# One core, attention then a relu² feed-forward: raw-weight loads of items 2 to 8 issued by GpSimd, and one accumulator of the last half kept in two PSUM tiles

## The chip, the core and the metric

The kernel runs on one core of a Trainium2 chip. The metric is device microseconds of one execution, lower is better. The three runs of the kernel before gave 591.52, 594.09 and 588.73 us, median 591.52 us. The profiled execution took 588.6 us.

Five engines work side by side: PE (TensorE: matrix products), DVE (VectorE), ACT (ScalarE), POOL (GpSimd) and SP (SyncE, which in this kernel issues every transfer). Each runs its own list of instructions in order, and waits at an instruction whose inputs or buffers are not ready. "SPq" in the profile is the issuing of a transfer.

## The reference

Attention over 4 batches, 8 heads, 768 positions of 64 features, with keys within a window of 16 positions and 24 block summaries (the maximum of each 32 keys; the mean of each 32 values). Its output, 3072 tokens of 512 features, goes through a feed-forward network of 2048 hidden features:

```
scores = concat(where(|i-j| < 16, q k^T / 8, -1e9), q ksum^T / 8 + log 32)
x = softmax(scores) @ concat(v, vsum)            # 3072 x 512
h = x @ w_in                                     # w_in 512 x 2048, float64
g = max(h, 0) ** 2
out = g @ w_out                                  # w_out 2048 x 512, float64
```

## The kernel before

**Tokens.** A group is 64 tokens of one batch (all heads): 48 groups. Eight groups make a unit of 512 tokens: 6 units. A group's attention is scores on PE (`S`, line 647), a maximum, exponential and normalisation on DVE and ACT (lines 739, 778, 797), a transposition, and the product with the values (line 854), which leaves x in `xh` and `xl`, a rounded high part and the remainder. The first eight groups take buffers that later hold weights (`qvpa_lent`, `fv_lent`).

**Block maxima of the keys.** `kb` holds 24 block maxima and then the keys. Scores read one run of columns, the maxima followed by 94 keys, so for each group POOL copies the maxima in front of the next window (`move`, line 660; called KC below). The scores of group g+1 read `kb` and wait for the KC of group g, which itself waits for the scores of group g. POOL also copies the value means into the value buffers of groups 0, 1, 6 and 7 (`copy_s`, line 605; called LS).

**Weights.** The 2048 hidden features are 16 items of 128. For an item, `convert` (lines 953 to 1021) loads 512 KB of w_in and 512 KB of w_out as raw 64-bit words (`load`, line 983: `raw<-wW`), and makes two float32 parts of each on chip: ACT line 986, DVE line 989 and line 995, ACT line 1000, DVE line 1003, whose output `w` PE reads. Items 0 to 2 are converted in two halves, the others whole. The raw words of items 6 to 15 lie in buffers that the first groups' attention used.

**Feed-forward.** Units 0 and 1 go item by item: `h = x w_in` on PE (line 1050, 12 matmuls), relu and square, then `o += g w_out` (line 1074, 12 matmuls). Units 2 and 3, and then 4 and 5, are computed with seven products for each 2 x 2 block in place of eight (`products(0, ...)` and `products(1, ...)`; line 1454). In `products` each of the seven steps j runs over 8 pairs of items and adds into a PSUM accumulator `o` of 128 x 2 x 512 (d = 0 and 1 are its halves of 512 columns, a PSUM bank each). The list `bank` says which accumulator step j uses. Steps 4 and 6 share the last one, `acc[4]`: step 4 fills it, DVE adds it to `u3` and the sum leaves (C22), step 6 adds eight pairs more, and DVE adds it to `u2` (C12, line 1400), whose two halves are the last two transfers of the program (line 1393). The very last pair of step 6 issues the three matmuls of d = 0 first, then the three of d = 1.

**Order.** A planner in Python (`Plan.order`) fixes the order of every engine's list ahead of time from estimated costs and due times (`due`, `begin`). A load is a task of SP there. All tasks are emitted in the planner's order, each on the engine that its lambda calls.

**Transfers.** SP's transfers use eight completion semaphores in turn, and the list makes each wait for the one eight before it. At most eight are therefore under way, and one that is not done holds back the ninth and all behind it.

Of the kernel before, what the change touches and what calls it, by code (L numbers as in the profile page):

```python
# [77 lines left out]
class Slots:  # L78


    def __init__(self, pool, tag, n, tiles=None):
        self.pool, self.tag, self.n, self.tiles = pool, tag, n, tiles
        self.taken, self.made = [], 0
# [21 lines left out]
class Part:  # L105
# [5 lines left out]
    @property  # L111
    def tile(self):
        x = self.buf.tile[:, self.a : self.b]
        return x.rearrange("p (a b) -> p a b", a=self.shape[1]) if self.shape else x
# [14 lines left out]
        return self.of(self.buf.tile)  # L129


class Task:
    def __init__(self, name, engine, cost, emit, key, after, take, use, size, begin):
        self.name, self.engine, self.cost, self.emit, self.key = name, engine, cost, emit, key
        self.after, self.size, self.begin = after, size, begin
        self.take, self.use = ([getattr(b, "buf", b) for b in x] for x in (take, use))


class Plan:
# [101 lines left out]
def attention_then_relu2_ffn(  # L241
# [9 lines left out]
    nc = tc.nc  # L251
# [3 lines left out]
    NT, DM = out.shape  # L255
# [21 lines left out]
    kinds = {}  # L277
# [61 lines left out]
    X_BY = 8  # L339
    SUMS = 274.9, 290.4, 308.3, 379.4, 174.9, 349.5, 257.2, 275.6, 114.0, 167.1, 155.4, 203.9, 122.9, 186.0, 213.8, 213.7  # L340
    BY_POOL = (1, 2, 4, 5,)
    PRODUCT_STEP = 1.56, 1.56, 1.46
    A0, A1, B0, B1 = 12.0, 2.0, 21.0, 2.2
    HALF_AT = 25.0, 32.0
# [2 lines left out]
    unit_at, products_at, at = [], [], T0  # L347
# [605 lines left out]
    def convert(f, ns):  # L953

        k = len(ns)  # L960
        due = at_item[0, f] + (LAG * STEP if ns == (1,) else 0)
        if f < HALVED:
            due = HALF_AT[0] + 0.5 * (f * SLOW + (LAG * STEP if ns == (1,) else 0))
        name = f"{f}" if k == 2 else f"{ns[0]}_{f}"

        raw = buf(f"w{name}", 1, (P, k * DM), I64, f"raw{name}")
        w = buf(f"w{name}", 1, (P, 2 * k * DM), F32R, f"w{name}")
        t = buf("t", 3, (P, 2 * DM), F32, f"t{name}")

        def temp():  # L970
            return t.tile[:, : k * DM]

        def words(i):
            return raw.tile.bitcast(U32).rearrange("p (c w) -> p c w", w=2)[:, :, i]

        def part(i, x):
            return x.rearrange("p (n w c) -> p n w c", n=k, w=2)[:, :, i]

        def by_n(x):
            return x.rearrange("p (n c) -> p n c", n=k)  # L980

        def load(i):
            nc.sync.dma_start(out=raw.tile[:, i * DM : (i + 1) * DM], in_=wW[ns[i], f])

        def rebias():
            nc.scalar.activation(temp(), words(1).bitcast(F32), AF.Prelu, scale=REBIAS, alpha=-SIGN)

        def rest():
            nc.vector.tensor_scalar(
                out=words(0), in0=words(0), scalar1=29, scalar2=None, op0=ALU.logical_shift_right  # L990
            )

        def join():
            x = temp().bitcast(U32)
            nc.vector.scalar_tensor_tensor(
                out=x, in0=x, scalar=3, in1=words(0), op0=ALU.logical_shift_left, op1=ALU.bitwise_or
            )

        def high():
            nc.scalar.copy(out=part(0, w.tile), in_=by_n(temp()))  # L1000

        def low():
            nc.vector.tensor_tensor(  # L1003
                out=part(1, w.tile), in0=by_n(temp()), in1=part(0, w.tile).bitcast(F32), op=ALU.subtract
            )

        t1 = []
        for i in range(k):
            t1.append(add(
                f"WL{ns[i]}_{f}", "SP", 0.45, lambda i=i: load(i), due - 14, take=[raw] * (not i), use=[raw] * i,  # L1010
                behind=t1[0] if i else None, size=P * 4096, begin=due - 31,
            ))
        t2 = add(f"WM{name}", "ACT", 0.02 + 0.5 * k, rebias, due - 8, t1, take=[t], use=[raw])
        t_WM.append(t2)
        t3 = add(f"WR{name}", "DVE", 0.09 + 0.27 * k, rest, due - 8, t1, use=[raw])
        t4 = add(f"WJ{name}", "DVE", 0.03 + 0.54 * k, join, due - 7, [t2, t3], use=[raw, t])
        t6 = add(f"WH{name}", "ACT", 0.08 + 0.43 * k, high, due - 6, [t4], take=[w], use=[t])
        t7 = add(f"WW{name}", "DVE", 0.07 + 0.53 * k, low, due - 4.5, [t6], use=[w, t])
        for i, n in enumerate(ns):
            t_W[n, f] = [t6, t7]  # L1020
            w_parts[n, f] = [Part(w, j * DM, (j + 1) * DM) for j in (2 * i, 2 * i + 1)]
# [351 lines left out]
    even, sums = {}, {}  # L1373

    def products(s, todo):

        if todo[0][:2] == (0, 0):
# [3 lines left out]
            if s:  # L1381
                sums[s][-1].update({("before", k): mixed_end[k] for k in range(2)})
        *acc, u2, u3, made = sums[s]
        bank = acc[0], acc[1], acc[2], acc[3], acc[4], acc[3], acc[4]

        def by_two(x):
# [2 lines left out]
        def leave(name, x, i, j, due, deps, d=slice(0, 2)):  # L1389
            c0 = s * 2 * TU + j * TU  # L1390
            rows = rest_out[i * HALF : (i + 1) * HALF, c0 : c0 + TU].rearrange("(d p) t -> p d t", p=P)
            add(
                f"PS{name}", "SP", 0.45, lambda: nc.sync.dma_start(out=rows[:, d], in_=by_two(x)[:, d]), due, deps, use=[x],
                size=(d.stop - d.start) * 4 * P * DM, begin=due - 20,
            )

        def plus(name, to, o, x, key, deps, take=(), d=slice(0, 2)):
            made[name] = add(
                f"{name}_{s}_{d.start}", "DVE", 0.13 + 0.56 * (d.stop - d.start),
                lambda: nc.vector.tensor_tensor(out=by_two(to)[:, d], in0=o.tile[:, d], in1=by_two(x)[:, d], op=ALU.add),  # L1400
                key, deps, take=take, use=[o, x] + [to] * (not take),
            )
            return made[name]

        for j, p, due in todo:
            o = bank[j]
# [4 lines left out]
            kind, c = ORDER[j]  # L1411
            x, ins, op = (
                (first, None, None), (second, None, None), (first, (last, first), ALU.add), (last, None, None),
                (diff, None, None), (second, (second, first), ALU.subtract), (diff, (first, diff), ALU.add),
            )[j]
# [7 lines left out]
                    out=chunk.tile.bitcast(F32), in_=of[c].rearrange("p w x -> p (w x)")  # L1423
# [4 lines left out]
            if op is not None:  # L1428
# [8 lines left out]
                take=[gh], use=[x], behind=last_of("gh", None) if n or s else t_FI[PLAIN, NF - 1],  # L1437
# [4 lines left out]
                    out=gl.tile, in0=x.tile, in1=gh.tile.bitcast(F32), op=ALU.subtract  # L1442
# [16 lines left out]
            for i, piece in enumerate((todo[::2], todo[1::2]) if end else (todo,)):  # L1459
                t_p = add(  # L1460
                    f"FP{s}_{n}_{i}", "PE", 0.2268 * len(piece), lambda piece=piece, mm=mm: mm(piece), due + 0.1 * i,
                    [t_h, t_l, t_c] + after, take=[o] * begins, use=[chunk, gh, gl] + [o] * (not begins),
                    behind=last_of("product", None),
                )
                last_of("product", t_p)
                if end:
                    d = slice(i, i + 1)
# [5 lines left out]
            if j == 0:  # L1473
                made["U1"] = add(
                    f"U1_{s}", "ACT", 0.97, lambda o=o: nc.scalar.copy(out=by_two(u2), in_=o.tile), due, [t_p], take=[u2], use=[o]
                )
            elif j == 1:
                x = buf("t", 3, (P, 2 * DM), F32, f"c11_{s}")
                leave(f"11_{s}", x, 0, 0, due + 1, [plus("C11", x, o, u2, due, [t_p, made["U1"]], [x])])
            elif j == 2:  # L1480
                plus("U2", u2, o, u2, due, [t_p, made["C11"]])
            elif j == 3:
                last_of("w1_1", plus("U3", u3, o, u2, due, [t_p, made["U2"]], [u3]))
            elif j == 4:
                leave(f"22_{s}", u3, 1, 1, due + 1, [plus("C22", u3, o, u3, due, [t_p, made["U3"]])])
                made["before", 5] = [made["U3"]]
            elif j == 5:
                x = buf("t", 3, (P, 2 * DM), F32, f"c21_{s}") if s else Buf(kinds["w1_2"], (P, 2 * DM), F32, f"c21_{s}")
                leave(f"21_{s}", x, 1, 0, due + 1, [plus("C21", x, o, u2, due, [t_p, made["U2"]], [x])])
                made["before", 6] = [made["C22"]]  # L1490
            elif not end:
                leave(f"12_{s}", u2, 0, 1, due + 1, [plus("C12", u2, o, u2, due, [t_p, made["C21"]])])

# [311 lines left out]
    for u in range(PLAIN + 2):  # L1805
# [14 lines left out]
        if u > PLAIN:  # L1820
            at, rest = unit_at[u], [(j, p) for j in range(SOON, PRODUCTS) for p in range(NQ)]
# [13 lines left out]
        o = [o_buf(f"o{u}_{t}") for t in range(NTT // 2)]  # L1835
# [76 lines left out]
```

## Time and profile before

| what | value |
|---|---|
| median of 3 runs | 591.52 us (588.73 to 594.09) |
| profiled execution | 588.6 us |
| its span, first to last instruction | 586.8 us |
| PE busy, share of the span | 573.3 us, 98% |
| DVE | 443.9 us, 76% |
| ACT | 353.0 us, 60% |
| POOL | 99.2 us, 17% |
| mean granted TensorE clock | 1.000 |
| moved by the transfers | 149.63 MB, 255 GB/s on average |

The 1.8 us between the span and the profiled execution's time lie outside the first and last instruction. PE is busy almost throughout, so the time is PE's work plus the places where PE waits. The profile names, for a wait, the instruction that ended it.

### The profile page before, as it was taken

The page shows a single profiled execution, that of the slowest core. Times are in us where ns is not written, and L with a number is a line of the kernel's source. Part 1 is how long each engine was busy: PE and PEld are TensorE (multiplying, and loading weights), DVE is VectorE, ACT ScalarE, POOL GpSimd, SP SyncE. Part 2 cuts the span into 40 slices and gives each one's busy share as a digit, 9 for nine tenths or more (in the row PEclk, how much of TensorE's full clock was granted, in tenths as well). Part 3 has the DMA queues.
Part 4 walks back from the last instruction along what each step waited for, and adds up shares of the span by engine and source line. Part 5 has one row for each costly group of instructions (what it writes and reads, how often), then busy time and mean ns, then how long its engine had stood idle before and what let it go on. Part 6 is the DMA issues. An engine that isn't in the chain of part 4 may idle for free.

```text
span 586.8 us, 12058 instructions
## 1 busy us (share of the span) xinstructions
PE 573.3 (98%) x4084; PEld 467.0 (80%) x4084; DVE 443.9 (76%) x1018; ACT 353.0 (60%) x876; POOL 99.2 (17%) x165
## 2 busy tenths in 40 slices
PE   8999999999999999999999999999999999999996
PEld 6787878777788888888778888888878888888885
DVE  5999899578457647765986877999968966769863
ACT  2999877667646646465754566676746424654442
POOL 4300005073568004420120022000000000000000
PEclk9999999999999999999999999999999999999999
DMA  8998885869998796996979945999885456667672
GB/s 313 324 394 304 304 301 161 289 214 336 356 325 261 235 332 201 322 320 185 268 248 296 363 153 183 295 303 287 271 268 178 122 158 194 197 187 232 196 225 99
DMA packets 120273, 149.63 MB, mean 255 GB/s; under 512 B 10556, under 2 KB 79164, under 8 KB 120212
## 3 DMA queue, kind: packets, MB, share of 16 engines
q1 hardware_dynamic: 120212, 148.86, 78.0%
q8 instruction: 33, 0.54, 0.4%
q14 instruction: 28, 0.23, 0.1%
HBM read 103.99 MB, written 44.04 MB: 252 GB/s over the span
## 4 chain that ended last, share of the span: by engine, by line
PE 71%; DMA 14%; DVE 5%; SPq 3%; ACT 3%; issue 2%; POOL 2%; DVEq 0%; ACTq 0%
PE o L1454 26%; PE h L1340 15%; PE o L1074 8%; PE o L1647 6%; DMA raw<-wW 6%; PE h L1050 6%; PE sz L1647 4%; PE x L854 3%; PE att L647 2%; DMA qvpa_lent<-vF 2%; DMA turn<-a 2%; DMA a<-turn 1%; PE att L1647 1%; DMA fv_lent<-vS 1%; DMA scr_i<-w 1%
## 5 line engine op out<-in xcount | busy, mean ns | idle before, releaser
L1454 PE MATMUL o<-gh,w 128*128 128x512 f32 x448 | 121.5, 393 | 0.0
L1436 ACT CAST gh<-g 128x512 fp32r<-128x512 f32 x112 | 68.5, 621 | 54.4 <-PE o L1454 25.2
L1454 PEld LDWEIGHTS o<-gh,w 128*128 128x128 f32 x448 | 83.1, 188 | 18.4 <-ACT gh L1436 0.8
L1441 DVE TENSOR_TENSOR gl<-g,gh 128x512 fp32r<-128x512 f32 x112 | 76.5, 695 | 20.9 <-ACT gh L1436 20.6
L1050 PE MATMUL h<-xh,w 128*128 128x512 f32 x240 | 75.0, 392 | 1.2 <-DVE w L1003 0.9
L1454 PE MATMUL o<-gl,w 128*128 128x512 f32 x224 | 69.5, 391 | 0.0
L1340 PE MATMUL h<-xh,w 128*128 128x512 f32 x224 | 69.1, 390 | 0.0
L1074 PE MATMUL o<-w,gh 128*128 128x512 f32 x240 | 62.2, 395 | 1.4 <-ACT gh L1061 1.2
L778 ACT ACTIVATE p<-p,small 128x118 f32<-128x118 f32 x160 | 61.0, 386 | 1.1 <-DVE small L721 0.7
L1050 PEld LDWEIGHTS h<-xh,w 128*128 128x128 f32 x240 | 44.7, 188 | 12.2 <-DVE w L1003 1.7
L1074 PEld LDWEIGHTS o<-w,gh 128*128 128x128 f32 x240 | 44.3, 188 | 11.8 <-ACT gh L1061 1.9
L1454 PEld LDWEIGHTS o<-gl,w 128*128 128x128 f32 x224 | 41.8, 188 | 9.6 <-DVE gl L1441 0.9
L1340 PEld LDWEIGHTS h<-xh,w 128*128 128x128 f32 x224 | 42.0, 188 | 9.1 <-ACT r L1350 0.4
L1050 PE MATMUL h<-xl,w 128*128 128x512 f32 x120 | 46.7, 389 | 0.0
L1340 PE MATMUL h<-xl,w 128*128 128x512 f32 x112 | 43.6, 389 | 0.0
L1350 ACT ACTIVATE r<-h 128x512 f32<-128x512 f32 x32 | 19.1, 596 | 37.1 <-PE h L1340 36.9
L660 POOL COPY kb<-kb 128x96 f32<-128x96 f32 x25 | 8.6, 343 | 193.3 <-ACT kw L672 70.9
L1064 DVE TENSOR_TENSOR gl<-r,gh 128x512 fp32r<-128x512 f32 x30 | 23.2, 774 | 20.3 <-ACT gh L1061 16.9
L721 DVE CUSTOM_DVE_ANT_0 p<-att,mask 128x118 f32<-128x118 f32 x152 | 33.1, 275 | 2.6 <-PE att L647 2.5
L1074 PE MATMUL o<-w,gl 128*128 128x512 f32 x120 | 33.6, 389 | 0.0
L1431 DVE TENSOR_TENSOR g<-g 128x512 f32<-128x512 f32 x48 | 32.8, 689 | 0.4
L778 ACT ACTIVATION_READ_ACCUMULATOR p<-p,small 128x1 f32 x160 | 30.4, 190 | 0.0
(209 smaller groups left out, 1077.7 us busy)
## 6 DMA issues: line engine op xcount, KB each, us to landing
raw<-wW SPq DMA_DIRECT2D x32, 512.0 KB
w<-scr_s SPq DMA_DIRECT2D x64, 256.0 KB
w<-scr_a SPq DMA_DIRECT2D x48, 256.0 KB
turn<-a SPq DMA_DIRECT2D x40, 256.0 KB
a<-turn SPq DMA_DIRECT2D x160, 64.0 KB
scr_t<-ci SPq DMA_DIRECT2D x32, 256.0 KB
w<-scr_i SPq DMA_DIRECT2D x32, 256.0 KB
w<-scr_t SPq DMA_DIRECT2D x32, 256.0 KB
```

The costliest lines, as they stand in the source:

```text
L721: nc.vector.tensor_tensor_reduce(out=pr.tile[:, j, :KEYS], in0=score_at(g, 0, j), in1=mask_of(g)[0], scale=-SCALE, scalar=-NEG, op0=ALU.ad ...
L778: nc.scalar.activation(x, score_tile(g, p % parts)[:, p] if by_pe else x, AF.Exp, bias=nm.tile[:, p : p + 1], scale=SCALE if by_pe else -1 ...
L1050: nc.tensor.matmul(cut(h), lhsT=lhs.tile[:, k * P : (k + 1) * P], rhs=rhs[:, k, c0 : c0 + n], start=(i == 0), stop=(i == 3 * KT - 1),)
L1064: lambda: nc.vector.tensor_tensor(out=cut(gl), in0=cut(r), in1=cut(gh).bitcast(F32), op=ALU.subtract),
L1074: nc.tensor.matmul(o_of(o, t), lhsT=terms[i][0].tile[:, (t - t0) * P : (t - t0 + 1) * P], rhs=terms[i][1].tile, start=(first and i == 0), ...
L1340: nc.tensor.matmul(h.tile, lhsT=lhs.tile[:, k * P : (k + 1) * P], rhs=rhs[:, k, c0 : c0 + TU], start=(i == 0), stop=(i == 3 * KT - 1),)
L1350: t2 = add(f"RL{name}", "ACT", 0.56, lambda: nc.scalar.activation(r.tile, h.tile, AF.Relu), due + 2 - R_LEAD, [t1], take=[r], use=[h])
L1431: lambda x=x, ins=ins, op=op: nc.vector.tensor_tensor(out=x.tile, in0=ins[0].tile, in1=ins[1].tile, op=op),
L1436: f"GH{s}_{n}", "ACT", 0.54, lambda x=x, gh=gh: nc.scalar.copy(out=gh.tile, in_=x.tile), due - GH_LEAD, ready,
L1441: lambda x=x, gh=gh, gl=gl: nc.vector.tensor_tensor(out=gl.tile, in0=x.tile, in1=gh.tile.bitcast(F32), op=ALU.subtract),
L1454: nc.tensor.matmul(o.tile[:, d], lhsT=chunk.tile[:, w * HALF + d * P : w * HALF + (d + 1) * P], rhs=y.tile, start=begins and w == 0 and y ...
L1647: nc.tensor.matmul(o.tile, lhsT=lhs(w, k), rhs=y[k], start=begins and i == 0, stop=i == 5, skip_group_check=not begins,)
```

## The change

There are two edits.

First, the transfers `raw<-wW` of items 2 to 8 (14 transfers of 512 KB) are issued by POOL and no longer by SP. In the planner they are still tasks of SP, so the order in which all tasks are emitted stays, and each of the 14 falls into POOL's list at the place that its emission gives it, between POOL's own copies. They use other completion semaphores than SP's.

Second, in `products(1, ...)` the accumulator of steps 4 and 6 consists of two PSUM tiles of 128 x 512, the two tiles that held the scores (`att`), in place of one tile of 128 x 2 x 512. The addition C22 becomes two instructions of 512 columns in place of one of 1024; C12 had two already.

```
+class Banks:
+    def __init__(self, bufs):
+        self.bufs = bufs
+    @property
+    def tile(self):
+        return self
+    def __getitem__(self, at):
+        d = at[1]
+        if isinstance(d, int):
+            return self.bufs[d].tile
+        assert d.stop == d.start + 1
+        return self.bufs[d.start].tile.unsqueeze(1)
...
+    RAW_BY_POOL = 2, 9
...
         def load(i):
-            nc.sync.dma_start(out=raw.tile[:, i * DM : (i + 1) * DM], in_=wW[ns[i], f])
+            (nc.gpsimd if RAW_BY_POOL[0] <= f < RAW_BY_POOL[1] else nc.sync).dma_start(out=raw.tile[:, i * DM : (i + 1) * DM], in_=wW[ns[i], f])
...
         *acc, u2, u3, made = sums[s]
+        if s and len(acc) == 6:
+            acc[4:] = [Banks([Buf(kinds["atts"], None, None, f"acc{s}_{d}") for d in range(2)])]
+            sums[s] = [*acc, u2, u3, made]
         bank = acc[0], acc[1], acc[2], acc[3], acc[4], acc[3], acc[4]
...
             elif j == 4:
-                leave(f"22_{s}", u3, 1, 1, due + 1, [plus("C22", u3, o, u3, due, [t_p, made["U3"]])])
-                made["before", 5] = [made["U3"]]
+                ds = [slice(d, d + 1) for d in range(2)] if s else [slice(0, 2)]
+                t_22 = [plus("C22", u3, o, u3, due, [t_p, made["U3"]], d=d) for d in ds]
+                leave(f"22_{s}", u3, 1, 1, due + 1, t_22)
+                made["before", 5], made["22"] = [made["U3"]], t_22
...
-                made["before", 6] = [made["C22"]]
+                made["before", 6] = made["22"]
```

On POOL, early in the program: in the rows, `kb<-kb` is a KC, `qvpa_lent<-fv_lent` an LS, and a number behind a name tells buffers apart (line numbers of the changed kernel are 19 or 22 higher). Before:

```order
L605 COPY qvpa_lent<-fv_lent 24x512
L660 COPY kb<-kb 128x4x24 x2
L605 COPY qvpa_lent<-fv_lent 24x512 x2
L660 COPY kb<-kb 128x4x24 x2
L710 MEMSET p_83 128x4x10
```

Now, from the same place:

```order
L679 COPY kb<-kb 128x4x24 x2
L1002 DMA raw_2_477<-wW 128x512
L624 COPY qvpa_lent<-fv_lent 24x512
L1002 DMA raw_496<-wW 128x512
L624 COPY qvpa_lent<-fv_lent 24x512
L1002 DMA raw_496<-wW 128x512
L1002 DMA raw_2_520<-wW 128x512
L1002 DMA raw_525<-wW 128x512
L679 COPY kb<-kb 128x4x24
L1002 DMA raw_525<-wW 128x512
L679 COPY kb<-kb 128x4x24
L729 MEMSET p_83 128x4x10
```

The first pair of `kb` copies are the KC of groups 4 and 5. Five transfers (item 2's two, item 3's two, one of item 4's) now stand between the KC of group 5 and that of group 6, and a sixth between those of groups 6 and 7. The other eight come later: two behind the KC of group 8, six behind that of group 9.

On SP, at the corresponding place, before:

```order
L983 DMA raw_1_459<-wW 128x512
L595 DMA v_80<-vF 128x512
L983 DMA raw_2_477<-wW 128x512
L595 DMA v_81<-vF 128x512
L983 DMA raw_496<-wW 128x512 x2
L983 DMA raw_2_520<-wW 128x512
L983 DMA raw_525<-wW 128x512 x2
L595 DMA v_82<-vF 128x512
L588 DMA q_617<-qW 128x256
```

Now:

```order
L1002 DMA raw_1_459<-wW 128x512
L614 DMA v_80<-vF 128x512
L614 DMA v_81<-vF 128x512
L614 DMA v_82<-vF 128x512
L607 DMA q_617<-qW 128x256
```

The loads of values and queries follow one another, and the same holds further down, up to the raw words of item 9, which SP still issues. On DVE, at the last additions, the rows before end in

```order
L1441 TENSOR_TENSOR gl_52_6397<-g_4_5171,gh_52_6395 128x512
L1441 TENSOR_TENSOR gl_53_6407<-g_5_5205,gh_53_6405 128x512
L1441 TENSOR_TENSOR gl_54_6417<-g_6_5274,gh_54_6415 128x512
L1441 TENSOR_TENSOR gl_55_6427<-g_7_5294,gh_55_6425 128x512
L1400 TENSOR_TENSOR u_1_5908<-o_66,u_1_5908 128x512 x2
```

and now in

```order
L1463 TENSOR_TENSOR gl_52_6398<-g_4_5171,gh_52_6396 128x512
L1463 TENSOR_TENSOR gl_53_6408<-g_5_5205,gh_53_6406 128x512
L1463 TENSOR_TENSOR gl_54_6418<-g_6_5274,gh_54_6416 128x512
L1463 TENSOR_TENSOR gl_55_6428<-g_7_5294,gh_55_6426 128x512
L1422 TENSOR_TENSOR u_1_5908<-att_68,u_1_5908 128x512
L1422 TENSOR_TENSOR u_1_5908<-att_69,u_1_5908 128x512
```

The two last additions read a tile each, and each has a wait for PE of its own; before, both read one tile, and the first waited for all of PE's work on it. PE's list is the same but for the names of the tiles that steps 4 and 6 write.

More of the change, by code (lines that the diff above doesn't have):

```diff
@@ L135, in __init__ @@
         self.after, self.size, self.begin = after, size, begin
-        self.take, self.use = ([getattr(b, "buf", b) for b in x] for x in (take, use))
+        self.take, self.use = ([getattr(c, "buf", c) for b in x for c in getattr(b, "bufs", (b,))] for x in (take, use))
 class Plan:
```

## The prediction

> **What bounds the kernel now.** I read the busy times by stage first, then who waits for whom on PE, then the order of time around PE's waits. Columns of the stages: busy us (instructions) on PE, weight loads, DVE, ACT, POOL, then granted clock, share of the transfer engines, GB/s.
>
> ```profile
> 0.00:20.00 20.00, 17.36 (x244) 13.44 (x244) 12.61 (x28) 7.83 (x31) 9.66 (x45) 1.00 0.92 327
> 20.00:40.00 20.00, 18.12 (x311) 15.57 (x312) 19.42 (x65) 19.28 (x72) 3.40 (x9) 1.00 0.96 356
> 40.00:60.00 20.00, 19.81 (x95) 15.87 (x97) 19.62 (x29) 19.19 (x37) 0.00 (x0) 1.00 0.93 323
> 60.00:80.00 20.00, 19.78 (x142) 16.10 (x135) 17.81 (x41) 14.72 (x34) 0.00 (x0) 1.00 0.92 322
> 200.00:300.00 100.00, 100.00 (x698) 81.41 (x697) 68.86 (x184) 56.15 (x152) 21.49 (x29) 1.00 0.85 274
> 560.00:587.00 27.00, 22.38 (x99) 18.20 (x97) 13.25 (x19) 8.73 (x14) 0.00 (x0) 1.00 0.49 157
> ```
>
> PE is full in the middle, where nothing but its own work counts. From 20 to 60 us DVE, ACT and the transfers are full as well: what is lost there on one of them has no slack to come out of.
>
> ```profile
> span 586.8 us, 12058 instructions
> PE 573.3 (98%) x4084; PEld 467.0 (80%) x4084; DVE 443.9 (76%) x1018; ACT 353.0 (60%) x876; POOL 99.2 (17%) x165
> ```
>
> All PE idle time is 586.8 - 573.3 = 13.5 us, and a good part of it lies before the first operands and behind the last matmul; that caps any gain.
>
> ```profile
> PE x L854 <- DMA a<-turn: 1.9, 3, 1.3
> PE o L1074 <- ACT gh L1061: 1.2, 1, 1.2
> PE h L1050 <- DVE w L1003: 0.9, 2, 0.7
> ```
>
> PE never waits for `raw<-wW` directly. It reaches PE through DVE's `w`, and that wait is 0.9 us in all, twice:
>
> ```profile
> 76.19 0.50 PE L1050 MATMUL h<-xh,w 128*128 128x512 f32 x1 [0.22 <-DVE w L1003]
> 82.59 0.50 PE L1050 MATMUL h<-xh,w 128*128 128x512 f32 x1 [0.66 <-DVE w L1003]
> ```
>
> **Edit 2, the end: -0.60 us.** The last rows before, on PE, DVE and SP:
>
> ```profile
> 581.31 0.39 PE L1454 MATMUL o<-gl,w 128*128 128x512 f32 x1
> 581.99 0.39 PE L1454 MATMUL o<-gl,w 128*128 128x512 f32 x1
> 582.41 1.29 DVE L1400 TENSOR_TENSOR u<-o,u 128x512 f32<-128x512 f32 x2 [3.19 <-PE o L1454]
> 583.13 0.93 SPq L1393 DMA_DIRECT2D out<-u  x2
> ```
>
> The matmul at 581.31 is the last of d = 0 and ends at 581.70. Its addition begins at 582.41 all the same, with the end of d = 1 (581.99 + 0.39 = 582.38). The pair takes 1.29 us. Of this the chain that ended last has 0.69 for the first addition and 0.60 for what the engine still did behind it:
>
> ```profile
> 582.41 0.69 DVE u L1400
> 583.11 0.60 DVEq L1908
> ```
>
> So the second adds 0.60 us. With a tile each, the first addition can start near 581.73 and end near 582.42, the second start near 582.42 and end near 583.11, not 583.70. The last transfer leaves 0.60 us sooner. Bounds: 0 if the first addition still waits, -0.69 if it vanishes wholly from the path. I take -0.60.
>
> C22 becomes two instructions: 2 x 0.69 - 1.23 = +0.15 us of DVE, where DVE was waiting for PE:
>
> ```profile
> 560.65 1.23 DVE L1400 TENSOR_TENSOR u<-o,u 128x1024 f32<-128x1024 f32 x1 [0.47 <-PE o L1454]
> ```
>
> The 0.47 us wait there covers it, and step 6, which needs C22, begins a whole step later. Cost 0; without that cover, 0.15.
>
> **Edit 1, the start: what 14 issues on POOL delay.** The queue moved from is SP's, the one moved into is POOL's, and what stands behind the new issues on POOL are the KC copies that scores on PE need. POOL before, and PE around it:
>
> ```profile
> 18.97 0.62 POOL L660 COPY kb<-kb 128x96 f32<-128x96 f32 x1 [0.50 <-PE o L647]
> 21.10 0.42 POOL L660 COPY kb<-kb 128x96 f32<-128x96 f32 x1 [1.50 <-PE o L647]
> 22.22 1.36 POOL L605 COPY qvpa_lent<-fv_lent 24x512 f32<-24x512 f32 x2 [0.70 <-DMA qvpa_lent<-vF]
> 23.71 0.49 POOL L660 COPY kb<-kb 128x96 f32<-128x96 f32 x1
> 26.13 0.27 POOL L660 COPY kb<-kb 128x96 f32<-128x96 f32 x1 [1.92 <-PE o L647]
> ```
> ```profile
> 20.11 0.43 PE L647 MATMUL o<-kb,qvpa_lent 64*64 64x118 f32 x8 [0.48 <-POOL kb L660]
> 25.13 0.43 PE L647 MATMUL o<-kb,qvpa_lent 64*64 64x118 f32 x8
> 25.79 0.38 PE L647 MATMUL o<-mask,unscale 64*64 64x118 f32 x8
> 27.07 0.63 PE L809 MATMUL t<-ident,qvpa_lent 128*128 128x128 f32 x4 [0.32 <-DVE qvpa_lent L797]
> 28.66 1.17 PE L854 MATMUL att<-qvpa_lent 118*64 118x64 f32 x32 [0.40 <-ACT qvpa_lent L816]
> 32.40 0.63 PE L809 MATMUL t<-ident,qvpa_lent 128*128 128x128 f32 x4 [0.54 <-ACT t L986]
> 35.45 0.39 PE L1050 MATMUL h_1a<-xh,w 128*128 128x256 f32 x1 [0.46 <-DVE w L1003]
> ```
>
> The KC at 23.71 is that of group 6, and the scores at 25.13 are those of group 7. Five issues now go ahead of that KC, between 21.52 (21.10 + 0.42) and it. No row shows an issue by POOL. Bounds of one: the shortest issue of the same transfer by SP, 0.32 us, and the longest POOL instruction on 128 x 512, 3.52 / 2 = 1.76 us.
>
> ```profile
> L983 SPq DMA_DIRECT2D raw<-wW x32: 323/431/1807, 15.6 to 104.6; - x32
> 93.39 3.52 POOL L1149 TENSOR_TENSOR cr<-w 128x512 f32<-128x512 f32 x2 [2.42 <-DVE w L1003]
> ```
>
> I take 0.68 us, a POOL copy at this very place (1.36 / 2): software work of POOL should be above SP's median of 0.431, and nothing is computed on the data. The KC of group 6 then ends at 21.52 + 5 x 0.68 + 1.36 + 0.49 = 26.77. From a KC's end to the scores it took 20.11 - (18.97 + 0.62) = 0.52, so the scores start at 27.29, 2.16 us late. The reader of these scores is DVE:
>
> ```profile
> 27.18 0.64 DVE L739 TENSOR_REDUCE small<-o 128x4 f32<-128x472 f32 x1
> 29.73 0.75 DVE L989 TENSOR_SCALAR raw<-raw 128x512 uint32<-128x512 uint32 x2
> ```
>
> It came 27.18 - (25.79 + 0.38) = 1.01 us after the scores' end. So DVE loses 2.16 - 1.01 = 1.15 us, and being full to 60 us it keeps that loss; PE's own extra 1.01 comes out of its four waits above (1.72 us in all), which were for DVE and ACT. The sixth issue delays the KC of group 7 no further: that one waits for the later scores, which take the same 0.66 + 0.38. The other eight issues have only the KC of groups 8 and 9 behind them, the first before two of them, the second needed near 60 us. Term: +1.15 us.
>
> By the Trainium skill, "DMA: Bandwidth & Descriptors", Specifications, the first byte of a GpSimd-issued transfer comes after about 1 us and that of an SP-issued one after about 0.6 us; with 1 us as the issue's length, an estimate by that page, five would take 5.0 in place of 3.4 us and the sum would be 1.6 us higher. No row here shows it.
>
> **Edit 1, the transfers themselves: +0.5 us.** The bytes are the same, and at 356 GB/s and 0.96 busy there is no idle transfer time between 20 and 40 us to win. A raw half of 524 KB takes 524 / 356 = 1.47 us of it. Issued beside SP's, the first two of POOL's (items 2 and 3) can come in ahead of item 1's last, up to 2 x 1.47 = 2.94 us, for which DVE waits at 29.73; 1.15 us of that is covered by DVE's own delay. Bounds 0 and 1.8. No raw wait shows there before, so I stay near the low end, 0.5.
>
> **Edit 1, what it gives back: -0.88 us.** The waits at 76.19 and 82.59 are for items 8 and 9, whose last DVE step stands behind four reductions that wait for the next batch's keys:
>
> ```profile
> DVE kb L479 <- DMA kb<-kT: 2.1, 3, 1.0
> ```
>
> Those keys shared SP's eight places and the transfer engines with item 9's raw words, which now go out earlier. And DVE's idle 20 - 17.81 = 2.19 us in that stage takes up its 1.15 us, while PE comes 1.15 us later. Either way 0.22 + 0.66 = 0.88 us goes. PE's other waits (1.2 for ACT, 1.9 for `turn`) hang on transfers behind PE's own progress and stay. Bounds 0 and -0.88 - 1.2.
>
> **Sum.** -0.60 + 1.15 + 0.50 - 0.88 = +0.17 us. On the profiled 588.6 us (span 586.8 and 1.8 us around it) that is 588.8. The median of the runs shown is 2.9 us above the profiled execution and they spread over 5.4 us; I set the sum on the median: 591.7 us. I call it the same: faster or slower means more than 1% (5.9 us), about what a measurement of this kernel can tell from no change.
>
> **Rivals.** First, POOL's issues are long, and KC is the new bound. A KC took 0.27 us at 26.13 and 0.62 at 18.97, with DVE at work in both: POOL's work can be stretched 2.3 times. An issue of 0.68 x 2.3 = 1.56 us moves the KC's end to 31.17 and the scores to 31.69, 6.56 us late; 6.56 - 1.01 - 0.88 - 0.60 = +4.1 us, 595.6. With 1.76 us it is +5.1, 596.6. The change loses from about 0.75 us per issue (0.65 with the 0.5 above), and passes 1% only beyond 1.9. Against it: nothing in these issues reads 512 columns. "SBUF — State Buffer", Who interferes with whom, in the Trainium skill, holds that GpSimd cannot write a transfer's descriptors while a DVE instruction in a two-port mode runs; line 989 would be such an instruction here, and no run shows it yet.
>
> Second, POOL's issues are short, as SP's: 0.43 x 5 = 2.15 us makes the scores 0.91 us late, inside DVE's 1.01. Then the loss is 0, and -0.60 - 0.88 = -1.5, 590.0; with the wait of 1.2 us for ACT gone too, -2.7, 588.8. For it: only the key copies are behind the issues. Against: no engine's row has POOL as fast as SP at this.
>
> Third, the first edit does nothing that counts: the transfers are bound by bandwidth at 0.96, the raw words land as before, the KC's delay and the regained 0.88 cancel. Then only the end is left, 590.9. Fourth, the end does not move, since the two additions still wait for one count of PE: 592.3 with the rest as forecast.
>
> **How the numbers follow.** Forecast 0.50, long issues 0.24, short issues 0.12, only the end 0.09, no gain at the end 0.05. The time is that of the forecast, 591.7. The range reaches up to long issues, 596.6 and 0.4 for the spread, 597.0, and down to the short ones with ACT's wait gone, 588.8, less the 2.8 us by which the runs shown fall below their median: 586.0. No case alone reaches -5.9 us; 0.07 for faster is left to the spread of the runs and to PE's other waits. Slower by more than 1% needs issues beyond 1.9 us or a late item 1 besides: 0.11. Same: 0.82.
>
> **What would show it.** POOL's rows should have five issues between 21.5 and 27 us of 0.6 to 0.8 us each, the scores of group 7 near 27.3 and not 25.13, DVE idle once near 27.2 for about 1.1 us, no waits for `w` near 76 and 83, and the last two additions apart, the first beginning before PE's last matmul. It is wrong if issues are over 1 us, if ACT or DVE wait for `raw` before 60 us, or if PE's waits behind 160 us change.

## The result and the profile after

The changed kernel is slower. Its median is 596.23 us (593.31 to 598.28, 10 runs), that of the kernel before 589.31 us (588.0 to 594.09, 10 runs). The ratio worked out over the runs is 1.0104 (the two medians alone give 1.0117), with a 95% interval of 1.0079 to 1.0128: +6.1 us, 4.7 to 7.5. The profiled execution took 598.28 us, 9.7 us more than that of before (588.6); section by section it reads as follows.

The head of the page, then the busy times by stage, in the columns of the prediction (PE, weight loads, DVE, ACT, POOL, granted clock, share of the transfer engines, GB/s):

```profile
span 596.5 us, 12076 instructions
PE 576.8 (97%) x4084; PEld 470.2 (79%) x4084; DVE 443.8 (74%) x1019; ACT 353.9 (59%) x876; POOL 107.6 (18%) x179
```
```profile
0.00:20.00 20.00, 17.37 (x244) 13.39 (x244) 12.19 (x28) 7.50 (x29) 9.66 (x45) 1.00 0.88 312
20.00:40.00 20.00, 14.28 (x248) 11.93 (x250) 14.20 (x42) 14.24 (x53) 7.55 (x16) 0.86 0.99 374
40.00:60.00 20.00, 19.63 (x126) 16.73 (x125) 19.49 (x46) 19.55 (x50) 3.58 (x7) 0.97 0.76 266
60.00:80.00 20.00, 20.00 (x144) 16.41 (x143) 17.50 (x38) 16.10 (x35) 0.00 (x0) 1.00 0.84 264
200.00:300.00 100.00, 99.59 (x751) 81.61 (x750) 67.72 (x197) 57.97 (x161) 20.00 (x28) 1.00 0.85 272
570.00:597.00 27.00, 22.30 (x99) 18.14 (x97) 13.32 (x20) 8.73 (x14) 0.00 (x0) 1.00 0.50 158
```

Most of the loss is in one stage, 20 to 40 us. PE is busy there for 14.28 us and not 18.12, DVE for 14.20 and not 19.42, ACT for 14.24 and not 19.28: all three wait, and PE's granted clock falls to 0.86. The transfers are a little busier than before (374 GB/s, 0.99). What comes after is later by as much, up to a further step behind 407 us.

PE runs the same 4084 matmuls in the same order in all the kernels here, so the start of the n-th can be set against that of the kernel before. This table is worked out from the traces of the profiled executions (start in us before, and us later in the changed kernel):

```
matmul   before   changed kernel
  300     22.71      0.33
  400     27.07      2.83
  450     29.61      2.80
  480     33.20      6.04
  640     59.77      6.24
 2000    246.23      6.29
 3200    407.05      6.26
 3600    472.51      9.93
 4083    581.99      9.92
```

There are two steps early, +2.5 us at about 25 us and +3.2 us at about 31 us, and in this profile no recovery up to 407 us. The step of 3.7 us between 407 and 472 us is in PE's waits for `turn` and `scr_i` transfers and a stretch at half clock behind them, none of which the change touches; over the other kernels below with the same code there, this stretch gave from -0.8 to +3.7 us, +1.0 in one that has both edits (e5). It is in e4 too (3.4), which has the first edit alone, and in e3 (2.8), which has the second alone, so it goes with the execution; without it the profiled ones would differ by some 6 us, where the medians differ by 6.9.

PE's waits in the two steps, and its later ones for `w`:

```profile
27.37 0.52 PE L666 MATMUL o<-kb,qvpa_lent 64*64 64x118 f32 x8 [1.97 <-POOL kb L679]
...
37.80 1.07 PE L828 MATMUL t<-ident,qvpa_lent 128*128 128x128 f32 x4 [3.15 <-DVE qvpa_lent L816]
...
82.51 0.50 PE L1069 MATMUL h<-xh,w 128*128 128x512 f32 x1 [0.28 <-DVE w L1022]
88.92 0.50 PE L1069 MATMUL h<-xh,w 128*128 128x512 f32 x1 [0.68 <-DVE w L1022]
```

The first step is the KC of group 6 on POOL. The issues, and the KC between them (26.80) and after (28.82):

```profile
21.99 0.70 POOL L1002 DMA_DIRECT2D raw<-wW  x1
23.33 0.87 POOL L624 COPY qvpa_lent<-fv_lent 24x512 f32<-24x512 f32 x1 [0.65 <-DMA qvpa_lent<-vF]
24.16 0.53 POOL L1002 DMA_DIRECT2D raw<-wW  x1
24.68 0.62 POOL L624 COPY qvpa_lent<-fv_lent 24x512 f32<-24x512 f32 x1
25.23 1.57 POOL L1002 DMA_DIRECT2D raw<-wW  x3
26.80 0.52 POOL L679 COPY kb<-kb 128x96 f32<-128x96 f32 x1
27.26 0.53 POOL L1002 DMA_DIRECT2D raw<-wW  x1
28.82 0.27 POOL L679 COPY kb<-kb 128x96 f32<-128x96 f32 x1 [1.03 <-PE o L666]
```

The KC ends at 27.32, where it had ended at 24.20, and the scores follow at 27.37. The second step is on DVE, which waits three times for raw words (27.54, 33.12 and 35.59), and never did so here before:

```profile
27.54 0.48 DVE L1008 TENSOR_SCALAR raw<-raw 128x512 uint32<-128x512 uint32 x1 [0.34 <-DMA raw<-wW]
29.11 0.65 DVE L758 TENSOR_REDUCE small<-o 128x4 f32<-128x472 f32 x1 [1.10 <-PE o L666]
33.12 0.43 DVE L1008 TENSOR_SCALAR raw<-raw 128x512 uint32<-128x512 uint32 x1 [1.40 <-DMA raw<-wW]
35.59 0.43 DVE L1008 TENSOR_SCALAR raw<-raw 128x512 uint32<-128x512 uint32 x1 [2.03 <-DMA raw<-wW]
```

Group 7's normalisation (line 816) stands behind these on DVE, and PE waits for that at 37.80. The raw words at 33.12 and 35.59 are the w_out halves of items 0 and 1, which SP still issues. From the trace's semaphore events:

```
                        issued   landed   took      (us)
before, item 0 w_out     24.00    28.03    4.0
before, item 1 w_out     24.57    29.42    4.9
after,  item 0 w_out     24.85    33.10    8.3
after,  item 1 w_out     25.42    35.56   10.1
after,  POOL's first 4   21.99 24.16 25.23 25.75, landed 26.11 30.32 34.74 36.66
```

The queues from 20 to 40 us (packets, MB, share of the engines), of the changed kernel and then of the kernel before, say why:

```profile
q1 hardware_dynamic: 1842, 3.64, 49.2%
q0 software_dynamic: 1032, 3.79, 48.6%
```
```profile
q1 hardware_dynamic: 2776, 7.06, 94.9%
```

With two queues full each got half: 3.64 MB for SP's, 3.79 for POOL's. A half that stood next in SP's single line now shares the engines with transfers that had stood behind it. The Trainium skill, "DMA: Bandwidth & Descriptors", Queues, rings and completion order, says that a transfer engine goes round the queues that hold work, a packet at a time. The 49.2% and 48.6% agree with the round; that it goes packet by packet the counts do not show (1842 and 1032, of different mean size).

There is a rival: POOL issued two halves (21.99, 24.16) before SP's first late one (24.85) and three before the second, so they might merely be served in the order of issue. At the prediction's 1.47 us for a half that is 2.9 and 4.4 us, and the two took 4.2 and 5.3 us longer than before. In e4 below, which has the same two queues, it is plainer: POOL's half of 24.00 landed at 32.63, ahead of SP's of 23.79 (33.85), and POOL's of 24.52 at 34.78, ahead of the load that SP issued at 24.26 (35.71). So the earlier issue is a part of it, but the order of issue alone does not give these landings. Nor is it the spread between executions: in the eight kernels here whose first such loads all go by SP in the old order (the one before, e1, e3, e6, e7, e9, e10, e11) the two halves took 4.0 to 6.0 and 4.9 to 6.7 us from issue to landing, and in the two with POOL's queue beside them (the changed one and e4) 8.2 to 8.3 and 10.1.

Behind each of the two waits PE ran at half clock (granted clock 0.50):

```profile
28.00:31.00 3.00, 3.00 (x36) 2.37 (x32) 1.83 (x7) 0.91 (x2) 0.33 (x2) 0.50 1.02 381
...
38.00:41.00 3.00, 3.00 (x42) 2.37 (x43) 3.00 (x7) 1.67 (x4) 0.58 (x2) 0.50 1.02 401
```

The end on PE, then C22 on DVE, then the last two additions on DVE:

```profile
591.46 0.62 PE L1476 MATMUL att<-gh,w 128*128 128x512 f32 x2
591.91 0.39 PE L1476 MATMUL att<-gl,w 128*128 128x512 f32 x1
```
```profile
570.36 0.69 DVE L1422 TENSOR_TENSOR u<-att,u 128x512 f32<-128x512 f32 x1 [0.24 <-PE att L1476]
...
571.56 0.68 DVE L1422 TENSOR_TENSOR u<-att,u 128x512 f32<-128x512 f32 x1
```
```profile
591.66 1.37 DVE L1422 TENSOR_TENSOR u<-att,u 128x512 f32<-128x512 f32 x2 [2.51 <-PE att L1476]
```

The first addition starts at 591.66, 0.25 us before PE's last matmul, and the pair ends at 593.03, 0.73 us behind PE's end (591.91 + 0.39 = 592.30). Before it was 583.70 against 582.38, 1.32 us: 0.59 us gained.

### The profile page after: what moved, and what is told of

Same layout as the page of the kernel before. It is cut to its first block, busy times and chain, and to the rows that moved or that the text cites. A ratio compares the mean times of both kernels' runs of the same rounds, so it can differ in the third digit from the quotient of the medians.

```text
span 596.5 us, 12076 instructions
## 1 busy us (share of the span) xinstructions
PE 576.8 (97%) x4084; PEld 470.2 (79%) x4084; DVE 443.8 (74%) x1019; ACT 353.9 (59%) x876; POOL 107.6 (18%) x179
## 4 chain that ended last, share of the span: by engine, by line
PE 78%; DMA 11%; DVE 4%; SPq 3%; issue 1%; ACT 1%; POOL 1%; DVEq 0%; ACTq 0%; POOLq 0%
PE o L1476 21%; PE h L1359 15%; PE o L1093 11%; PE h L1069 8%; PE o L1671 6%; DMA raw<-wW 5%; PE sz L1671 4%; PE att L1476 4%; PE x L873 3%; PE att L666 3%; DMA q<-qW 2%; DMA v<-vS 2%; PE o L666 2%; PE att L1671 1%; DMA kb<-kT 1%
## 5 line engine op out<-in xcount | busy, mean ns | idle before, releaser
L1476 PE MATMUL o<-gh,w 128*128 128x512 f32 x384 | 104.0, 392 | 0.0
L1476 PEld LDWEIGHTS o<-gh,w 128*128 128x128 f32 x384 | 71.3, 188 | 15.5 <-ACT gh L1458 0.3
L1476 PE MATMUL o<-gl,w 128*128 128x512 f32 x192 | 59.5, 391 | 0.4 <-DMA q<-qW 0.4
L1476 PEld LDWEIGHTS o<-gl,w 128*128 128x128 f32 x192 | 35.9, 188 | 8.8 <-DVE gl L1463 1.3
```

The costliest lines, as they stand in the source:

```text
L1476: nc.tensor.matmul(o.tile[:, d], lhsT=chunk.tile[:, w * HALF + d * P : w * HALF + (d + 1) * P], rhs=y.tile, start=begins and w == 0 and y ...
```

## The experiments

Theory A: the two early steps are two costs, the KC's delay by POOL's issues and the late w_out halves, and the second comes from two queues taking turns. Theory B: all of it is the issues' time on POOL. Ratios are to the kernel before on the same chip, with 95% intervals; a thousandth is 0.59 us. The last two columns are from one profiled execution of each.

| kernel | median us | ratio | interval | PE later at 60 us | at 407 us |
|---|---|---|---|---|---|
| changed kernel | 596.23 | 1.0104 | 1.0079 to 1.0128 | 6.2 | 6.3 |
| e3, second edit alone | 589.08 | 0.9972 | 0.9947 to 0.9998 | 1.3 | -0.7 |
| e4, first edit alone | 594.95 | 1.0093 | 1.0061 to 1.0124 | 4.2 | 2.6 |
| e7, POOL's delay alone | 592.00 | 1.0029 | 1.0009 to 1.0050 | 2.4 | 3.1 |
| e1, the same with a new tile | 597.33 | 1.0117 | 1.0090 to 1.0144 | 3.2 | 8.1 |
| e8, late halves alone | 595.30 | 1.0078 | 1.0052 to 1.0103 | 6.1 | 3.8 |
| e2, halves later still | 598.01 | 1.0134 | 1.0101 to 1.0167 | 9.2 | 9.4 |
| e5, halves by POOL too | 593.37 | 1.0064 | 1.0035 to 1.0093 | 4.6 | 3.7 |
| e6, POOL for items 5 to 8 | 591.62 | 1.0013 | 0.9989 to 1.0037 | 1.0 | 3.1 |
| e12, ACT in POOL's place | 598.65 | 1.0138 | 1.0079 to 1.0197 | 9.4 | 8.8 |
| e10, keys by POOL | 588.85 | 0.9974 | 0.9947 to 1.0001 | 0.8 | -0.1 |
| e9, last fetches by POOL | 593.44 | 1.0051 | 1.0030 to 1.0073 | 1.1 | 0.3 |
| e11, e9 and e10 | 592.22 | 1.0029 | 1.0005 to 1.0053 | 0.3 | -3.7 |

All but e4 have the two tiles at the end.

**e3 and e4: one edit each.** e3 sets `RAW_BY_POOL = 99, 99`; e4 leaves the accumulator one tile:

```
-        if s and len(acc) == 6:
+        if False:
...
-                ds = [slice(d, d + 1) for d in range(2)] if s else [slice(0, 2)]
+                ds = [slice(0, 2)]
```

> Only the second edit: all raw words by SP, the last accumulator in two tiles. Both theories: -0.6 us on the kernel before, from the last addition alone; the first of the two last additions begins about 0.3 us before PE's last matmul. A rival that puts part of the loss on the second edit expects +1 us or more, with longer PE waits near 440 us.

> Only the first edit: POOL issues the raw words of items 2 to 8, one accumulator tile as before. Both theories: the loss of the changed kernel and 0.6 us more, about +6.7 us on the kernel before, with PE waits of 2 us near 27 and 3 us near 38, each followed by some 3.4 us at half clock. The rival that blames the second edit expects less than +5 us.

e3 gave -1.6 us (-0.1 to -3.1), which holds the expected 0.6; its end is 0.73 us behind PE's, as in the changed kernel. e4 gave +5.5 us. The second edit is no part of the loss. One point of e4 was missed: its profile has no 2 us wait for a KC. There POOL's copies of means did not wait and the KC of group 6 ended at 25.85, so nearly all of its 4.2 us came in the second step, a PE wait of 4.47 us at 36.09:

```profile
25.57 0.28 POOL L679 COPY kb<-kb 128x96 f32<-128x96 f32 x1
```
```profile
36.09 0.63 PE L828 MATMUL t<-ident,qvpa_lent 128*128 128x128 f32 x4 [4.47 <-DVE qvpa_lent L816]
```

How the loss divides between the two steps changes from execution to execution.

**e7 and e1: the delay without the transfers.** SP issues everything, and POOL clears a small tile at the same places, meant to take an issue's length. e1 used a new tile of 192 bytes in four clears, e7 the existing `scratch` in five:

```
+            if RAW_BY_POOL[0] <= f < RAW_BY_POOL[1]:
+                for _ in range(5):
+                    nc.gpsimd.memset(scratch, 0.0)
+            nc.sync.dma_start(out=raw.tile[:, i * DM : (i + 1) * DM], in_=wW[ns[i], f])
```

> SP issues every transfer as before; at each of the 14 places where the changed kernel issues on POOL, POOL clears a tile four times (about 0.54 us, an issue's 0.55), so the KC of group 6 is as late as in the changed kernel (26.8 us) and nothing else competes. The two tiles at the end stay. Theory A (the loss is in the transfers: POOL's queue takes turns with SP's, and the w_out halves of items 0 and 1 come late): the first PE wait (about 2 us near 27) and the half clock behind it come back, but DVE does not wait for raw words; +1 to +2.5 us on the kernel before. Theory B (the loss is in the KC's delay by the issues): about the whole loss of the changed kernel, +6 us.

> POOL is kept busy as long at the 14 places by five small clears of a tile that exists anyway (about 0.55 us), SP issues every transfer, and no tile's address changes (the earlier delay kernel had a new tile of 192 bytes ahead of many others). Theory A: PE is 2.5 to 3.3 us late at 40 us, keeps that, and no DVE wait for raw words comes; +1.5 to +3 us on the kernel before. Theory B (the issues' time alone makes the loss): +6 us. If the shift of addresses was what made PE lose 4 us more behind 120 us in the earlier delay kernel, PE's lateness at 330 us is within 0.5 us of that at 60 us here.

e7, on POOL and PE, and its clock:

```profile
24.43 2.49 POOL L1004 MEMSET small<- 128x16 f32 x15
26.87 0.54 POOL L679 COPY kb<-kb 128x96 f32<-128x96 f32 x1
```
```profile
27.46 0.43 PE L666 MATMUL o<-kb,qvpa_lent 64*64 64x118 f32 x8 [2.57 <-POOL small L1004]
```
```profile
28.00:31.00 3.00, 3.00 (x32) 2.37 (x31) 1.90 (x7) 0.81 (x3) 0.44 (x3) 0.50 1.02 380
```

Five clears took about 0.8 us here and not an issue's 0.53, but POOL's copies of means waited less (0.15 us and not 0.65), so the KC comes at the same time as in the changed kernel (27.41 and 27.32). The first step is there, with the half clock behind it; the second is not. PE is 2.4 us late at 60 us, and the time is +1.7 us (0.5 to 3.0), 3.4 us above e3. So the delay is a real cost, but not the whole: theory B falls. e1 agreed with B at first sight (+6.9 us), but its PE was only 3.2 us late at 60 us and then lost 5 us more, little by little, between 120 and 407 us, where POOL does nothing new. e7 lost 0.7 us from 60 to 330 us (0.5 was the bound set for it) and e1 4.4.

**e8 and e2: the late halves without POOL.** SP issues all, with the w_out halves of items 0 and 1 behind two (e8) or four (e2) halves of items 2 and 3:

```
+            if f < 2 and ns == (1,):
+                held.append(issue)
+                return
+            issue()
+            gone.extend([f] * (f in (2, 3)))
+            while held and len(gone) == 2:
+                held.pop(0)()
```

> POOL issues nothing. SP issues all, but the w_out halves of items 0 and 1 go out behind four halves of items 2 and 3, so that they land near 34 and 36 us as in the changed kernel; no KC is late. The two tiles at the end stay. Theory A: DVE waits for raw words near 30 to 36 us by about 3 to 5 us, PE waits 3 us behind it, the clock falls once; +3 to +5 us on the kernel before. Theory B: the late halves cost nothing, only the end is left, -0.6 us.

> POOL issues nothing; SP issues the w_out halves of items 0 and 1 behind only two halves of items 2 and 3, so that they land near 34.5 and 35.8 us, as in the changed kernel (33.1 and 35.6). No KC is late. Theory A: PE is 4 to 5.5 us late at 40 us from a DVE wait for raw words alone and keeps it; +3 to +5 us on the kernel before. Theory B: no loss, -0.6 us or the -1.6 us that the two tiles at the end gave alone.

In e8 the halves landed at 33.95 and 35.18 us, close to the changed kernel's. DVE and PE:

```profile
33.97 0.43 DVE L1017 TENSOR_SCALAR raw<-raw 128x512 uint32<-128x512 uint32 x1 [3.70 <-DMA raw<-wW]
35.20 0.43 DVE L1017 TENSOR_SCALAR raw<-raw 128x512 uint32<-128x512 uint32 x1 [0.80 <-DMA raw<-wW]
```
```profile
37.41 1.09 PE L828 MATMUL t<-ident,qvpa_lent 128*128 128x128 f32 x4 [4.90 <-DVE qvpa_lent L816]
```

The KC of group 6 is not late (it ends at 24.21), DVE waits 4.5 us, PE 4.9, and the time is +4.6 us (3.1 to 6.1), 6.3 above e3. The late halves are the larger cost. The two parts (3.4 and 6.3) make more than the changed kernel's 7.8 us above e3. That fits, though it was not tried by itself: the wait for the KC lies ahead of the wait for the halves on DVE and covers part of it. e2 put the halves further back than intended: they landed at 37.0 and 38.3 us, PE waited 8.95 us, and the loss was above what was expected of it.

**e12: another second queue.** `nc.scalar` in place of `nc.gpsimd`.

> The changed kernel with ACT in place of POOL as the issuer of the raw words of items 2 to 8 (14 issues of about 0.4 us in ACT's list, which is full from 20 to 60 us); no KC is late. What it is to tell: whether the w_out halves of items 0 and 1, on SP, come late beside any second queue or only beside POOL's. Theory A (any two queues take turns): they land at 31 to 36 us and DVE waits for them by 1 us or more. Rival (only transfers that POOL issues do this): they land at 28 to 30 us as in the kernel before. Either way the time is at least 2 us above the kernel before, since ACT loses its issues' time.

The halves landed at 30.63 and 33.12 us, 6.9 and 8.9 us after their issue and longer than in the eight kernels with SP alone in the old order, with two of ACT's transfers in ahead of them (30.30 and 32.81). The queues from 20 to 40 us (q10 is ACT's):

```profile
q1 hardware_dynamic: 1695, 3.43, 47.2%
q10 hardware_dynamic: 908, 3.33, 47.0%
```

Half each again, so this is two queues and not something of POOL. The expected DVE wait for the halves did not come, since ACT itself stood longer: it waited 5.0 us in two places for raw words to land, between its own issues, and DVE waited for ACT:

```profile
34.00 0.17 DVE L809 TENSOR_SCALAR small<-small 128x4 f32<-128x4 f32 x1 [7.32 <-ACT qvpa_lent L797]
```

**e5: all raw words in one line.** The w_out halves of items 0 and 1 go by POOL too.

```
-            (nc.gpsimd if RAW_BY_POOL[0] <= f < RAW_BY_POOL[1] else nc.sync)...
+            (nc.gpsimd if RAW_BY_POOL[0] <= f < RAW_BY_POOL[1] or (f < 2 and ns == (1,)) else nc.sync)...
```

> The changed kernel with the w_out halves of items 0 and 1 issued by POOL too, ahead of item 2, so that all raw words stand in one line again, and two more issues (1.1 us) ahead of the KC of group 6. Theory A: the halves land near 29 to 31 us, DVE waits for raw words under 1 us, the KC is later than in the changed kernel by about 1.1 us; PE 3 to 4.5 us late at 40 us; +2.5 to +4 us on the kernel before, so 2 to 3 us faster than the changed kernel. Theory B: 1.1 us or more slower than the changed kernel, +7 us.

They landed at 26.70 and 28.28, earlier than in any other kernel here, and the time fell by 2.4 us against the changed kernel (the two intervals overlap a little), although the KC came still later (27.71). But DVE did wait, for more than the 1 us expected at most:

```profile
31.27 0.43 DVE L1008 TENSOR_SCALAR raw<-raw 128x512 uint32<-128x512 uint32 x1 [3.04 <-DMA raw<-wW]
```

This is the w_in half of item 1, now the last of the early ones left to SP: issued at 23.34, landed at 31.25 (before 21.33 and 25.54). The lateness moved to the transfer that stayed behind in the other queue.

**e6: only items 5 to 8 by POOL.** `RAW_BY_POOL = 5, 9`.

> POOL issues only items 5 to 8 (8 transfers, all behind the KC of group 8), SP items 2 to 4; two tiles at the end. Theories A and B: no KC of groups 6 and 7 late, w_out halves of items 0 and 1 in time, so the time of the two tiles alone, 0 to -2 us on the kernel before. Against both: +2 us or more, if issuing by POOL costs wherever it stands, or if the two queues take turns to the harm of items 3 and 4.

+0.8 us (-0.6 to +2.2), and 2.4 above e3: neither early step is there, but issuing by POOL gains nothing later either. The value lies between the two that were expected. The profile has PE 1.0 us late at 60 us and 2.9 at 166, with waits of 1.45 and 1.41 us for ACT near 97 and 112; what made them was not separated.

**e9, e10 and e11: the same means where it might help.** In e3, POOL takes the `a<-turn` loads of groups 44 to 47, the keys of batch 1, or both.

```
-                    nc.sync.dma_start(
+                    (nc.gpsimd if g >= 44 else nc.sync).dma_start(
...
-            nc.sync.dma_start(out=kb[:, p, NB:], in_=kT[b, p * P : (p + 1) * P, :])
+            (nc.gpsimd if b == 1 else nc.sync).dma_start(out=kb[:, p, NB:], in_=kT[b, p * P : (p + 1) * P, :])
```

> The two tiles at the end, raw words by SP, and the 16 transfers a<-turn of groups 44 to 47 (415 to 440 us) issued by POOL, which has nothing else then. Theory A (two queues take turns, so a transfer on the emptier queue passes those waiting in the other): PE's waits for a<-turn between 430 and 450 us (1.6 us in the profile of the kernel before, up to 4 us in the others) fall under 0.5 us; with the two tiles -2.5 to -5 us on the kernel before. Rival: the issue by POOL (0.55 us each, or more for this shape, 2.2 us for four) takes as long as the queueing it saves: no change to the two tiles alone, 0 to -2 us.

> The two tiles at the end, raw words by SP, and the four key loads kb<-kT of the second batch issued by POOL (idle from 31 to 90 us). Theory A: the keys land 2 to 4 us sooner than at 67.5 to 72.6 us, DVE's four reductions do not wait (2.1 us before), PE's waits for w of items 8 and 9 (0.22 + 0.66 us) go: -1 to -2.5 us on the kernel before. Rival: those waits come from DVE's own order and stay: the two tiles alone, 0 to -2 us, or a loss if the raw words of items 9 to 11 land later.

> The last two kernels' moves together with the two tiles. Theory A: the sum, -3 to -6 us on the kernel before, all by transfers that go past a backlog and none that is put ahead of an urgent one. Rival: no better than the two tiles alone, 0 to -2 us.

e10 is e3's time. POOL issued the keys 1.8 to 2.7 us sooner than SP had, and they landed at the same time, 68.2 to 72.5 us (before 67.5 to 72.6), so it seems that the busy transfer engines held them and not SP. In e11's profile they landed at 66.1 to 70.1, and PE was 3.7 us early at 407 us; one execution does not tell whether the move did that. e9 and e11 lost 4.7 and 3.4 us to e3. PE in e9, and the transfers' median time to landing:

```profile
435.21 0.69 PE L873 MATMUL x<-a,v 118*64 118x64 f32 x16 [4.00 <-DMA w<-scr_i]
```
```profile
a<-turn POOLq DMA_DIRECT2D x16, 64.0 KB, 5.3
```

The wait is put down to `w<-scr_i`, but the last `a<-turn` of that group landed at 434.96, and PE went on at 435.21. For this group it took from the landing of `turn<-a` to that of the last `a<-turn` 5.1 us before, 7.4 in e9 and 8.0 in e11. So theory A's corollary, that a transfer on the emptier queue goes past the others, failed for these small ones. Why they took longer on POOL's queue was not separated: four issues of 0.55 us in a row are part of it, and the rest stays open.

## Why the prediction was right and where it was wrong

The measured time lies in the range, but 4.5 us above the forecast; as a difference, +0.2 us was forecast and +6.1 came. That the range holds it is luck: its upper end, 597.0, was set by long issues on POOL, which did not happen. The ratio of 1.0104 also lies just past the prediction's own line of 1% between "same" and "slower" (the interval has both). "Slower" got 0.11, for issues beyond 1.9 us "or a late item 1 besides", and the late item is what came.

**The end: right.** -0.60 predicted, -0.59 in the trace, and C22's two additions (0.69 and 0.68) cost nothing visible.

**POOL's issue: right in place, somewhat short in time.** 0.68 us was taken; the fourteen took 0.53 us in the middle and 0.70 at most. The KC's end was put at 26.77 and came at 27.32 (the copies of means waited 0.65 us and the execution was 0.33 us later from the start), the scores at 27.29 and came at 27.37. The rule of the Trainium skill, "SBUF — State Buffer", Who interferes with whom, that DVE holds up GpSimd's descriptors does not show: no issue was stretched to 1.56 us. "Long issues", the rival that gave 595.6, is refuted, although its number is near the measured one.

**What the KC's delay costs: mis-sized.** 1.15 us was predicted; e7 has PE 2.4 us late. Two things were left out. PE's extra was to come out of its 1.72 us of waits. In e7 the first three of them (1.26 us) are indeed gone, but after its wait of 2.57 us PE ran 3 us at 0.50, which is 1.5 us of its work, and that took what they gave. And the scores behind the wait were to take "the same 0.66 + 0.38" = 1.04 us; partly at half clock they took 1.52 in e7 (27.46 to 28.98) and 1.70 in the changed kernel (27.37 to 29.07). So they ended 2.8 and 2.9 us late and not 2.16, and, with the 1.01 us of slack taken off, DVE's reduction came 1.86 and 1.93 us late (29.04 and 29.11 for 27.18) and not 1.15.

**The competition: the step that failed.** The term was +0.50 us with a bound of 1.8; e8 and the second step of the changed kernel put it at 3.2 to 6.1 us. The argument counted two POOL transfers ahead of item 1's last, as if they were to join one line. In fact the queues each got half of the engines for as long as both were full, so three of POOL's raw halves and most of a fourth (26.11 to 36.66) came in ahead of SP's second, and SP's two landed 5.1 and 6.1 us later than before (33.10 for 28.03, 35.56 for 29.42), 0.85 of it because they were issued later. "No raw wait shows there before" was true, and no evidence: the halves had landed 1.7 and 0.7 us ahead of their use by DVE (29.73 and 30.1 us), and any lateness beyond that would show. The full transfers (0.96) were read as no idle transfer time "to win"; they should have been read as a sign that only the order can change.

**What it gives back: wrong.** 0.88 us was to return at 76 and 83 us. The waits are still there, at 82.51 and 88.92, 0.28 and 0.68 us: PE and the chain of weights both moved by 6.3 us, so a gap between them stayed. The item's raw words do not decide it: those of item 8 were in by 52.4 us, and the keys that DVE waits for landed 6.3 to 7.3 us later than before. The term is not nothing in every kernel, though: PE's waits between 60 and 166 us are 2.7 us before and 2.9 in the changed kernel, but 0.5 in e3 and 0.9 in e8, whose PE regained 3.0 and 2.2 us there. What decides it stays open.

**Of the signs named in advance,** five issues before the KC, scores near 27.3, a DVE wait of about 1.1 us for them (1.10, though at 29.11 and not 27.2) and the early addition at the end came true (the issues took 0.53 to 0.70 us, a little under the 0.6 to 0.8 named); that no waits for `w` would be left did not. "If ACT or DVE wait for `raw` before 60 us" was named as a mark of a wrong forecast, and it came. So did the third mark, a change in PE's waits behind 160 us (3.9 us for 1.6), but by the step that goes with the execution.

The second edit alone (e3) is 1.6 us (0.1 to 3.1) faster than the kernel before. The end gives 0.6 of that; the rest is not explained.

## What to carry to other kernels

Where the transfers are full, as here, a second queue brings no bandwidth; it changes who is served, and here it was half and half between the queues. Before some transfers are moved to another engine, look for the urgent ones that stay in the first queue: they are the ones that pay, and their slack (landing against first use) is the bound. An in-order engine that issues for others delays what stands behind on its own list by the issues' time, where it had no wait there that hides them, and PE can pay for a wait of 2 us a second time in clock.

## What the runs showed of the hardware

An issue of the same 512 KB takes POOL 0.53 us and SP 0.43 us in the middle (shortest, median and longest ns, in the changed kernel):

```profile
L1002 SPq DMA_DIRECT2D raw<-wW x18: 328/432/752, 16.1 to 110.6; - x18
L1002 POOL DMA_DIRECT2D raw<-wW x14: 527/528/697, 22.0 to 43.7; - x14
```

A wait of 1.97 us was enough for the granted clock to go from 1.00 to 0.50, for 3 us (28 to 31 us in the rows above). "TensorE: Matmul & The Clock Gate" in the Trainium skill, Part 1, speaks of an idle window of about 3.4 us for this; here less idle time did it. The length of one wait does not settle it: in e3 a wait of 1.76 us (to 420.16) was followed by half clock, in e1 one of 2.14 (to 98.70) was not. In the 16 places between 20 and 585 us where the clock fell in these traces, PE had been idle for 1.6 to 3.4 of the 3.4 us ahead of the fall, and it stayed at 0.50 for 3.4 us or a multiple.

e1 and e7 differ by the new tile of 192 bytes, which moved the tiles behind it, and by how the clears were cut. The same matmuls took 3 ns more each between 170 and 330 us in e1 (first row) than in e7 (second):

```profile
L1363 PE MATMUL h<-xh,w 128*128 128x512 f32 x144 | 44.8, 392 | 0.1
```
```profile
L1362 PE MATMUL h<-xh,w 128*128 128x512 f32 x151 | 46.6, 389 | 0.0
```

Over all matmuls of 512 columns there (605 and 614) the mean is 393.6 ns against 391.2, some 1.5 us, of the 2.8 us that e1 lost to e7 between the 1400th and the 2600th. That the addresses are the cause was not tried by itself.
